# Two head groups of x in one pass over eight TensorE tiles, with w_val's sum and one residual per batch on GpSimd

## The chip, the core and the metric

The kernel runs on one core of one Trainium2 chip. The metric is device time in microseconds (us); the time before is the median of three runs, 319.11 us (318.81 to 319.12). Every view of the profile is of one profiled execution of the kernel before, whose own time is 318.79 us. A time "at 86.9" is counted from the first instruction of that execution.

The engines, as the profile names them: PE is TensorE's matmuls and PEld its weight loads, DVE is VectorE, ACT is ScalarE, POOL is GpSimd, SP is the engine from whose queue all DMAs are issued. PSUM is the memory that matmuls write, SBUF the one that everything else uses.

## The reference

Inputs: q, k, v of 8 batches x 8 heads x 576 rows x 64; p of 8 x 8 x 32 x 64; float64 weights w_val and w_out of 512 x 512 and conv_w of 5 x 512. (q, k, v and p arrive as float32.)

```python
def sm_attn(qq, kk, vv):
    s = scale * np.matmul(qq, kk.transpose(0, 1, 3, 2))
    a = np.exp(s - np.max(s, axis=-1, keepdims=True))
    a = a / (np.sum(a, axis=-1, keepdims=True) + 1e-09)
    return np.matmul(a, vv)
p_packed = sm_attn(p, k, v)              # 32 packed rows per head
out = sm_attn(q, p_packed, p_packed)     # 576 rows per head
x = out.transpose(0, 2, 1, 3).reshape(B, S, H * D)     # 8 x 576 x 512
for k in range(5):
    gate_pre += conv_w[k] * xp[:, k:k + S, :]          # xp: x behind 4 rows of zeros
gate = 1.0 / (1.0 + np.exp(-gate_pre))
return gate * (x @ w_val) @ w_out
```

## The kernel before

One batch's work is cut into streams, each a Python generator: loads (K, V, Q, P for a batch's tensors, L for the weights), `keys` k, `attn_pack` a, `queries` q, `packed_turned` p, `attn_out` s, `weighted` t, `packed_values` w, `mixed` x, `gate` g, `value` v and `project` o, and once per kernel the weights' conversion from float64 words: `value_weights` W, `conv_weights` C and `out_weights` O. The table ORDER is a list of tokens such as `x0` (one step of `mixed` for batch 0) or `a0.3` (three steps of `attn_pack` for batch 0). A step is what stands between two `yield`s. Each engine is wrapped in `InOrder`, so the order in which the tokens issue instructions is the order in which each engine, and the DMA queue of SP, runs them. What moves work is therefore ORDER together with the code of the streams and the numbers of buffers (NB in SBUF, PSB in PSUM).

The eight heads of a batch are two groups of four (G is 2, g counts them). A group's four heads lie on the partitions 0-31, 32-63, 64-95 and 96-127 of `a2` (the weights of the second attention, transposed) and of `ppd` (the packed rows).

The steps that the change touches:

- `words_of`, `from_double`, `summed`, `value_weights`: w_val comes as pairs of 32-bit words in four chunks of 128 rows. ACT and DVE turn a chunk into a high part (`wv_top`) and a low part (in `wv_words`). PE adds the two through matmuls with the identity (`wv_sum`), ACT copies the sum to `wv`. `wv` is read by `packed_values` (`wp`), which gives `wph` and `wpl`, the operands of `value`.
- `weighted`: DVE sums, takes reciprocals, POOL multiplies (`t<-t,rs`), DVE transposes to `a2` (named a in the profile), ACT and DVE split it into `a2h` and `a2l`.
- `mixed`: for each group and each half of the 576 columns four matmuls of 32 x 64 weights and 288 columns, one per head, write x transposed to one PSUM buffer; ACT copies it to `xp`. Head hl takes the rows 32 hl of TensorE's array and the columns 64 (hl mod 2), so four of the eight tiles of that shape are in use at a time:

```python
xps[D * (hl % 2) : D * (hl % 2) + D, hl // 2, :HS],
pp[heads[hl], g, 0, :],
a2[heads[hl], g, hc],
```

- `gate`: from `xp`, one ACT and four DVE instructions for each of four 128-channel blocks, then tanh on ACT, in the tile `sig`.
- `value`: 12 matmuls per block into one PSUM buffer (`val`), DVE multiplies with the gate (`sig<-sig,val`), ACT rounds to `gvh`, and DVE takes the rest, `gvl<-sig,gvh`.
- `project`: output chunks of 128 rows, 36 matmuls each over `gvh`, `gvl`, `woh` and `wol` (o), copied by ACT and written by DMA. For the last batch five chunks are accumulated side by side.

The PSUM buffers called `big` hold two banks each, and there are two of them: scores (s), `wp`, x and `val` take turns in them. Three `mid` buffers and one `out` buffer serve the rest.

Of the kernel before, what the change touches and what calls it, by code (L numbers as in the profile page):

```python
# [9 lines left out]
F32 = mybir.dt.float32  # L10
U32 = mybir.dt.uint32
F32R = mybir.dt.float32r
AF = mybir.ActivationFunctionType
ALU = mybir.AluOpType
# [25 lines left out]
 'xp': 2}  # L40
# [66 lines left out]
def packed_attention_gated_conv(  # L107
# [38 lines left out]
    DM = H * D  # L146
# [27 lines left out]
    eps = const.tile([P, G * NBLK], F32, name="eps")  # L174
# [56 lines left out]
    def from_double(nm, words, rows):  # L231
# [6 lines left out]
        yield  # L238
        dve.tensor_scalar(hw, hw, 1 << 31, None, op0=ALU.bitwise_and)
# [167 lines left out]
    def weighted(b):  # L407
# [5 lines left out]
        for gs in parts(b):  # L413
# [4 lines left out]
            dve.tensor_tensor(s3, s3, eps[:, : n * NBLK], op=ALU.add)  # L418
# [32 lines left out]
    def mixed(b):  # L451

        for g in range(G):
# [3 lines left out]
            for half in range(2):  # L457
                hc = slice(half * HS, half * HS + HS)
                pp, a2 = st["ppd", b], st["a2", b]
                xps = big(f"x_{b}_{g}_{half}")  # L460
# [8 lines left out]
                yield  # L469
                act.copy(xp[:, :, half, PAD:], xps[:, :, :HS])  # L470
# [32 lines left out]
    def value(b):  # L503
        base = (b % 2) * S
        wph, wpl, ah, al = (st[nm, b] for nm in ("wph", "wpl", "ah", "al"))
        for n4 in range(NC):
            vps = big(f"val_{b}_{n4}")
            cols = slice(n4 * P, n4 * P + P)
            for half in range(2):
                hc = slice(half * HS, half * HS + HS)  # L510
                n = 0
                for g in range(G):
                    for w, x in ((wph, ah), (wpl, ah), (wph, al)):
                        pe.matmul(
                            vps[:, half, :HS], w[:, g, cols], x[:, g, hc], start=(n == 0), stop=(n == 5)
# [10 lines left out]
            dve.tensor_tensor(  # L526
# [119 lines left out]
```

## Time and profile before

| | |
|---|---|
| median of three runs | 319.11 us |
| the profiled execution: time, span from first to last instruction | 318.79 us, 316.7 us |
| busy, of the span: PE, DVE, ACT, POOL | 292.0, 256.5, 211.1, 44.8 us |
| granted TensorE clock, mean | 0.997 |
| HBM read, written | 33.57 MB, 9.44 MB |

How to read it: a matmul's busy time runs from its start to its modelled end, and neighbours overlap in it. Where the prediction needs the time that a step takes up on an engine it uses the chain of work that ended last, whose pieces do not overlap: each line there is a start, a length and what ran. A row of the groups by line gives operation, output and inputs by their names in the program, shapes, count, busy time in all, the mean of one in ns, and the idle time before them with what ended it. A row of the table by stretches gives the stretch, its length, each engine's busy time with its number of instructions, the granted clock, the share of the DMA engines and GB/s. All instructions bear line 90, that of the helper that issues them, so the names tell them apart. A matmul in float32 is two instructions in the profile: x8 is four matmuls.

### The profile page before, as it was taken

How to read it: one execution, taken by the hardware profiler on the slowest of the kernel's cores; microseconds unless marked ns; L12 is line 12 of the kernel's file. 1: busy time of each engine (PE TensorE's matmuls, PEld its weight loads, DVE VectorE, ACT ScalarE, POOL GpSimd, SP SyncE). 2: the span in 40 equal slices, each digit the busy share in tenths (PEclk: the TensorE clock that was granted, in tenths of full speed). 3: DMA queues.
4: the chain of work that ended last, by engine and by line, in shares of the span. 5: the costliest groups of instructions: out<-in, count | busy, mean ns of one | idle time of the engine just before them, and what ended most of it. 6: DMA issues, size and time to landing. Idle time of an engine off the chain costs nothing.

```text
span 316.7 us, 7391 instructions
## 1 busy us (share of the span) xinstructions
PE 292.0 (92%) x3028; PEld 210.3 (66%) x3028; DVE 256.5 (81%) x404; ACT 211.1 (67%) x428; POOL 44.8 (14%) x55
## 2 busy tenths in 40 slices
PE   0878987988899999999999999999999999999992
PEld 0534534556766876787777867777787687767871
DVE  0336799999888987898999888997999878868761
ACT  1564787688966778768867786688766955455431
POOL 1000131113002210033003202210032100220000
PEclk9999999999999999999999999999999999999998
DMA  8999999999991479328652866415242021111005
GB/s 180 220 231 226 243 256 218 214 229 192 192 198 74 107 188 224 83 81 216 151 139 73 208 185 120 123 55 129 58 141 68 2 66 36 66 68 47 20 2 167
DMA packets 42476, 43.50 MB, mean 137 GB/s; under 512 B 6085, under 2 KB 36805, under 8 KB 42442
## 3 DMA queue, kind: packets, MB, share of 16 engines
q1 hardware_dynamic: 42442, 43.02, 58.8%
q8 instruction: 24, 0.39, 0.6%
q14 instruction: 10, 0.08, 0.1%
HBM read 33.57 MB, written 9.44 MB: 136 GB/s over the span
## 4 chain that ended last, share of the span: by engine, by line
PE 69%; DVE 15%; ACT 6%; DMA 5%; issue 1%; SPq 0%; POOL 0%; POOLq 0%; DVEq 0%; ACTq 0%
PE o L90 26%; PE val L90 13%; DVE sig L90 6%; PE s L90 5%; PE x L90 5%; PE kpt L90 4%; PE qpt L90 4%; PE pv L90 3%; DMA qm<-in_q_dram 3%; PE at L90 3%; PE wv_sum L90 2%; PE wp L90 2%; DMA p<-in_p_dram 2%; DVE sm L90 2%; ACT sig L90 2%; DVE wo_words L90 1%
## 5 line engine op out<-in xcount | busy, mean ns | idle before, releaser
L90 DVE SCALAR_TENSOR_TENSOR sig<-xp,cw,sig 128x576 f32<-128x576 f32 x128 | 107.5, 840 | 5.9 <-ACT sig L90 4.8
L90 PE MATMUL o<-woh,gvh 128*128 128x512 f32 x144 | 59.0, 409 | 0.1
L90 PE MATMUL o<-wol,gvh 128*128 128x512 f32 x144 | 56.5, 393 | 0.0
L90 PE MATMUL o<-woh,gvl 128*128 128x512 f32 x144 | 56.5, 392 | 0.1
L90 PE MATMUL val<-a2h,wph 128*128 128x288 f32 x128 | 39.9, 312 | 0.0
L90 POOL TENSOR_TENSOR t<-t,mx 128x576 f32<-128x576 f32 x16 | 22.9, 1432 | 110.3 <-DVE mx L90 110.3
L90 PE MATMUL val<-a2h,wpl 128*128 128x288 f32 x128 | 37.9, 296 | 0.0
L90 PE MATMUL val<-a2l,wph 128*128 128x288 f32 x128 | 37.8, 295 | 0.0
L90 ACT COPY osb<-o 128x512 f32<-128x512 f32 x34 | 19.9, 584 | 25.1 <-PE o L90 17.0
L90 ACT ACTIVATE sig<-sig 128x576 f32<-128x576 f32 x32 | 22.0, 689 | 21.3 <-DVE sig L90 21.3
L90 DVE SCALAR_TENSOR_TENSOR sig<-sig,val 128x576 f32<-128x576 f32 x32 | 24.0, 751 | 12.6 <-ACT sig L90 7.8
L90 PEld LDWEIGHTS o<-woh,gvh 128*128 128x128 f32 x144 | 27.1, 188 | 8.8 <-ACT osb L90 2.4
L90 PEld LDWEIGHTS o<-woh,gvl 128*128 128x128 f32 x144 | 27.1, 188 | 6.7 <-DVE gvl L90 0.5
L90 PEld LDWEIGHTS o<-wol,gvh 128*128 128x128 f32 x144 | 27.1, 189 | 4.6
L90 PEld LDWEIGHTS kpt<-ident,km 96*128 96x128 f32 x192 | 20.2, 151 | 11.9 <-issue 4.8
L90 ACT COPY qT<-qpt 128x384 f32<-128x384 f32 x48 | 23.2, 486 | 6.8 <-PE qpt L90 6.5
L90 ACT CAST gvh<-sig 128x576 fp32r<-128x576 f32 x32 | 21.6, 676 | 9.0 <-DVE sig L90 7.9
L90 POOL TENSOR_TENSOR t<-t,rs 128x576 f32<-128x576 f32 x16 | 19.9, 1244 | 54.6 <-DVE rs L90 47.3
L90 PE MATMUL kpt<-ident,km 96*128 96x96 f32 x192 | 25.7, 266 | 2.0 <-DVE wol L90 1.0
L90 DVE TENSOR_TENSOR gvl<-sig,gvh 128x576 fp32r<-128x576 f32 x32 | 24.6, 769 | 2.5 <-ACT gvh L90 2.3
L90 PEld LDWEIGHTS val<-a2h,wph 128*128 128x128 f32 x128 | 24.2, 189 | 2.7 <-issue 0.9
L90 ACT COPY kT<-kpt 128x384 f32<-128x384 f32 x48 | 22.9, 483 | 4.2 <-PE kpt L90 4.0
(82 smaller groups left out, 504.9 us busy)
## 6 DMA issues: line engine op xcount, KB each, us to landing
km<-in_k_dram SPq DMA_DIRECT2D x16, 576.0 KB, 6.1
qm<-in_q_dram SPq DMA_DIRECT2D x16, 576.0 KB, 7.0
vm<-in_v_dram SPq DMA_DIRECT2D x16, 576.0 KB, 7.3
out_dram<-osb SPq DMA_DIRECT2D x24, 256.0 KB, 2.1
wv_words<-in_moe_w_val_dram SPq DMA_DIRECT2D x8, 256.0 KB, 9.1
wo_words<-in_moe_w_out_dram SPq DMA_DIRECT2D x4, 512.0 KB, 13.6
out_dram<-osb SPq DMA_DIRECT2D x8, 192.0 KB, 3.4
p<-in_p_dram SPq DMA_DIRECT2D x16, 64.0 KB, 7.9
```

The lines of the kernel that those rows point to most:

```text
L90: made = getattr(self.engine, op)(*args, **kw)
```

## The change

- `mixed` issues both groups for one half in one step, each group into a PSUM buffer of its own, the second group with its two column halves swapped (`at = D * ((hl + g) % 2)`). The eight matmuls so name all eight tiles of 32 rows x 64 columns. ACT copies the two buffers in two further steps. `xp` has three buffers instead of two, `mx2` two instead of three, and `eps` half its size.
- The channels of group 1 lie swapped by this; the rows or columns of w_val, conv_w and w_out are swapped to match, as they are loaded (`halves`, two small DMAs for conv_w) or written (`wv`).
- `value_weights`: the sum of the two parts is two POOL additions of 128 x 256 per chunk instead of two matmuls and an ACT copy.
- `value`: for the first of the four blocks (n4 is 0) `gvl` is computed by POOL, for the others by DVE as before.
- ORDER is another table from the first token to the last.

`from_double` also gets two arguments that no call uses.

```diff
- 'xp': 2}
+ 'mx2': 2,
+ 'xp': 3}
...
-x0 K0.2 P0 L0.2 Q0 L0.2 V0.2 k0 Q0 L0 k0.2 P1 k0.4 P2 W0 k0.2 W0 K1 k0.2 a0 W0 k0.2 W0 a0 k0 K1 W0.2 a0 W0 L0 a0
+x0 L0 x0 K0 L0 P0 L0 K0 W0 L0 W0.2 P1 W0.2 L0 W0 V0 W0 Q0 V0 W0 k0 Q0 W0 k0.2 P2 W0 k0.2 W0 L0 k0.2 W0.2 K1 k0
...
+    def halves(c):
+        return (c * P, c * P + D) if c < NC // 2 else (c * P + D, c * P)
...
-        st["words", "cw"] = words_of("cw", [conv_w], NT)
+        st["words", "cw"] = words_of("cw", [conv_w[:, : DM // 2]], NT, DM // 2)
+        swapped = conv_w[:, DM // 2 :].bitcast(U32).rearrange("n (c t d) -> n c t d", c=2, t=2)
+        to = st["words", "cw"][:, DM // 2 :, :].rearrange("n (c t d) x -> n c t (d x)", c=2, t=2)
+        for t in range(2):
+            sp.dma_start(to[:, :, t], swapped[:, :, 1 - t])
...
-            st["words", "wo"][c] = words_of(f"wo{c}", [w_out[c * P : c * P + P, :]], P)
+            st["words", "wo"][c] = words_of(f"wo{c}", [w_out[r : r + D, :] for r in halves(c)], P)
...
-            ps = summed(f"wv{c}", words)
-            yield
-            act.copy(wv[:, c, :], ps)
+            for low in range(2):
+                cs = slice(low * DM // 2, low * DM // 2 + DM // 2)
+                to = wv[:, c, cs].rearrange("a (x t d) -> a x t d", x=2, t=2)
+                ins = [
+                    x[:, cs].rearrange("a (x t d) -> a x t d", x=2, t=2)
+                    for x in (st["top", f"wv{c}"], words[:, :, 0].bitcast(F32))
+                ]
+                pool.tensor_tensor(to[:, :, ::-1] if low else to, *ins, op=ALU.add)
...
+        for half in range(2):
+            hc = slice(half * HS, half * HS + HS)
+            pp, a2 = st["ppd", b], st["a2", b]
+            xps = [big(f"x_{b}_{g}_{half}") for g in range(G)]
+            for g in range(G):
                 for hl in range(4):
+                    at = D * ((hl + g) % 2)
                     pe.matmul(
-                        xps[D * (hl % 2) : D * (hl % 2) + D, hl // 2, :HS],
+                        xps[g][at : at + D, hl // 2, :HS],
...
+            for g in range(G):
+                act.copy(st["xp", b, g][:, :, half, PAD:], xps[g][:, :, :HS])
                 yield
...
-            dve.tensor_tensor(
+            (pool if n4 == 0 else dve).tensor_tensor(
                 lo, gv, hi.bitcast(F32), op=ALU.subtract
             )
```

How the instructions stand, at three places. First PE at the start, from the second attention product of batch 0's first group (`pv_0`) on: `at` are transposes for it, `qpt` and `pTt` transposes of q and p, `ppTt` that of the packed rows, `s_0_0` the scores that begin batch 0's second attention, `wp` the product with w_val. Before:

```order
L90 MATMUL at_1_2_306<-ident,a_0_1_223 96x128 x2
L90 MATMUL pv_1_310<-vm_1_103,a1t_1_294 32x64 x24
L90 MATMUL wv_sum<-wv_top,ident 128x512
L90 MATMUL wv_sum<-wv_words,ident 128x512
L90 MATMUL qpt_1_0_350<-ident,qm_1_108 128x96 x4
L90 MATMUL ppTt_356<-ident,ppd_226 128x128 x2
L90 MATMUL pTt_359<-ident,p_120 128x128 x2
L90 MATMUL qpt_1_1_369<-ident,qm_1_108 128x96 x4
L90 MATMUL s_0_0_379<-qT_0_199,ppT_363 32x288 x8
```

And now:

```order
L91 MATMUL at_1_2_329<-ident,a_0_1_241 96x128 x2
L91 MATMUL cwps<-ident,cw_top 128x5 x4
L91 MATMUL pv_1_338<-vm_1_122,a1t_1_317 32x64 x24
L91 MATMUL ppTt_365<-ident,ppd_244 128x128 x2
L91 MATMUL qpt_1_0_373<-ident,qm_1_128 128x96 x4
L91 MATMUL s_0_0_380<-qT_0_294,ppT_370 32x288 x8
```

The last `wv_sum` no longer stands between `pv_1` and `ppTt`, and one `qpt` instead of two and `pTt` stands ahead of the scores.

Second, PE in batch 6 around its x (`x_0_1` is group 0, half 1; `pv`, `at` and `qpt` there belong to batch 7, `val` to batch 5). Before:

```order
L90 MATMUL x_0_1_3300<-a_6_3164,ppd_2670 64x288 x4
L90 MATMUL pv_0_3307<-vm_0_2903,a1t_0_3255 32x64 x24
L90 MATMUL qpt_1_1_3335<-ident,qm_1_3104 128x96 x4
L90 MATMUL at_1_0_3344<-ident,a_7_1_3237 96x128 x2
L90 MATMUL wp_3347<-wv,ppT_3062 32x512 x8
L90 MATMUL x_1_0_3364<-a_6_3164,ppd_2670 64x288 x4
```

And now:

```order
L91 MATMUL val_1_3272<-a2l_2685,wph_2678 128x288
L91 MATMUL x_0_0_3287<-a_6_3147,ppd_2648 64x288 x4
L91 MATMUL x_1_0_3288<-a_6_3147,ppd_2648 64x288 x4
L91 MATMUL pv_0_3299<-vm_0_2886,a1t_0_3122 32x64 x24
L91 MATMUL x_0_1_3327<-a_6_3147,ppd_2648 64x288 x4
L91 MATMUL x_1_1_3328<-a_6_3147,ppd_2648 64x288 x4
L91 MATMUL val_2_3343<-a2h_2684,wph_2678 128x288
```

The four x of a batch, which stood apart, stand in two pairs with only `pv_0` between them, and `val` directly ahead of and behind them.

Third, POOL from batch 6's last multiplication (`t<-t,rs`) to the end. Before:

```order
L90 TENSOR_TENSOR t_6_3068<-t_6_3068,rs_6_3163 128x576
L90 MEMSET xp_1_3356 128x4x2
L90 MEMSET xp_0_3467 128x4x2
L90 TENSOR_TENSOR t_7_3564<-t_7_3564,mx_7_3565 128x576
L90 TENSOR_TENSOR t_7_3564<-t_7_3564,rs_7_3635 128x576
L90 TENSOR_TENSOR t_7_3564<-t_7_3564,mx_7_3565 128x576
L90 TENSOR_TENSOR t_7_3564<-t_7_3564,rs_7_3635 128x576
L90 MEMSET xp_1_3718 128x4x2
```

And now:

```order
L91 TENSOR_TENSOR t_6_3055<-t_6_3055,rs_6_3146 128x576
L91 TENSOR_TENSOR gvl<-sig_0_2945,gvh 128x576
L91 MEMSET xp_0_3361 128x4x2
L91 TENSOR_TENSOR t_7_3430<-t_7_3430,mx_7_3431 128x576
L91 TENSOR_TENSOR t_7_3430<-t_7_3430,rs_7_3510 128x576
L91 MEMSET xp_1_3532 128x4x2
L91 TENSOR_TENSOR gvl<-sig_0_3368,gvh 128x576
L91 TENSOR_TENSOR t_7_3430<-t_7_3430,mx_7_3431 128x576
L91 TENSOR_TENSOR t_7_3430<-t_7_3430,rs_7_3510 128x576
L91 TENSOR_TENSOR gvl<-sig_0_3685,gvh 128x576
```

Three `gvl` (of the batches 5, 6 and 7) have come into the queue, and batch 7's second subtraction stands behind batch 6's `gvl`.

More of the change, by code (lines that the diff above doesn't have):

```diff
@@ new lines @@
+t4 a5 k6 a5 q5 k6 o2 v3 q5 t4 g3 v3 t4 x4 g3 o2 t4 k6 o2 v3 q5 x4 K7 a5 g3 x4 Q6 v3 t4 a5 k6 q5 g3 a5 v3 g3 x4
+v3 V6 a5.3 v3 k6 x4 a5.2 v3 a5 g4 k6 g4 x4 x5 a5 v3 k6 a5.2 k6 g4 v3 k6 g4 a5 a6 V6 k6 K7 p5 v3 k7 o3 p5 a6 g4
+a6 g4.2 s5 o3 g4 a6 o3 s5 o3 k7 a6 s5 a6 g4 s5 a6 g4 w5 o3.2 s5.2 a6 w5 t5 k7 q6 o3 a6 k7 g4 t5 q6 s5 g4 w5 g4
+x5 q6 g4 o3 v4 q6 o3 t5 g4 t5 o3 s5 g4 s5 t5 q6 s5 k7 Q7 a6 q6 t5 o3 q6 a6 o3.2 q6 g4 t5 k7 v4 g4.2 t5 v4 a6 g4
+o3 x5 v4 t5 o3 g4 k7 a6.2 x5.3 V7 a6 k7.2 a6 x5 g4 a6 q6 k7 v4 t5 q6 a6 g4 x5 k7 g4 x6 v4 a6 q6 g5 Q7 v4 g5 k7
@@ L79 @@
+v6.2 o5 g6 o5 t7 g6 o5 g6 v6 t7 g6 v6.3 o5 g6 o5 t7 x7 g6 t7 g6 x7.2 t7 x7 g6 x7 v6 x7 v6 g7 v6 o6 g7 v7 o6 g7
+o6 g7 o6 g7.3 v7 g7 v7 o6 g7 v7.2 o6.2 g7.2 o6 g7 o6.2 g7 v7 g7 v7.3 g7 o6 g7 o6 o7 g7.3 v7 g7 v7 o7 v7 g7.3 o7
+g7 v7 o7 v7.3 o7.15
 """
@@ L173, in packed_attention_gated_conv @@
     heads = [slice(NP * hl, NP * hl + NP) for hl in range(4)]
-    eps = const.tile([P, G * NBLK], F32, name="eps")
+    eps = const.tile([P, NBLK], F32, name="eps")
     nc.gpsimd.memset(eps, 1e-9)
@@ L204, in load_q, with words_of @@
         yield from load(b, "q", q, "h (a i c) d -> i h a (c d)")
-    def words_of(nm, src, rows):
+    def halves(c):
+        return (c * P, c * P + D) if c < NC // 2 else (c * P + D, c * P)
+    def words_of(nm, src, rows, cols=DM):
         words = tile_of("words", [P, DM, 2], U32, f"{nm}_words", stage)[:rows]
@@ L212, in words_of @@
             sp.dma_start(
-                words[n * each : n * each + each].rearrange("a b c -> a (b c)"), s.bitcast(U32)
+                words[n * each : n * each + each, :cols].rearrange("a b c -> a (b c)"), s.bitcast(U32)
             )
@@ L227, in load_weights, with from_double @@
         for c in range(NC):
-            st["words", "wo"][c] = words_of(f"wo{c}", [w_out[c * P : c * P + P, :]], P)
+            st["words", "wo"][c] = words_of(f"wo{c}", [w_out[r : r + D, :] for r in halves(c)], P)
             yield
-    def from_double(nm, words, rows):
+    def from_double(nm, words, rows, by=1.0, rest_on_pool=False):
         top = st["top", nm] = tile_of("top", [P, DM], F32, f"{nm}_top", stage)[:rows]
@@ L238, in from_double @@
         yield
+        if rest_on_pool:
+            act.mul(rest, lw, 2.0**-52 * by)
+            yield
         dve.tensor_scalar(hw, hw, 1 << 31, None, op0=ALU.bitwise_and)
@@ L246, in from_double @@
         yield
-        dve.scalar_tensor_tensor(
-            rest, lw, 2.0**-52, hw.bitcast(F32), op0=ALU.mult, op1=ALU.mult
-        )
+        if rest_on_pool:
+            pool.tensor_tensor(rest, rest, hw.bitcast(F32), op=ALU.mult)
+        else:
+            dve.scalar_tensor_tensor(
+                rest, lw, 2.0**-52 * by, hw.bitcast(F32), op0=ALU.mult, op1=ALU.mult
+            )
         yield
@@ L417, in weighted @@
             dve.tensor_reduce(s3, t3, axis=AX.X, op=ALU.add)
[L418 removed]
+            dve.tensor_tensor(s3, s3, eps, op=ALU.add)
             dve.reciprocal(r3, s3)
@@ L456, in mixed @@
             yield
[L457 to L460, printed above, removed]
+        for half in range(2):
[3 more added lines that the diff above has]
+            for g in range(G):
                 for hl in range(4):
+                    at = D * ((hl + g) % 2)
                     pe.matmul(
-                        xps[D * (hl % 2) : D * (hl % 2) + D, hl // 2, :HS],
+                        xps[g][at : at + D, hl // 2, :HS],
                         pp[heads[hl], g, 0, :],
@@ L468, in mixed @@
                     )
-                yield
-                act.copy(xp[:, :, half, PAD:], xps[:, :, :HS])
+            yield
+            for g in range(G):
+                act.copy(st["xp", b, g][:, :, half, PAD:], xps[g][:, :, :HS])
                 yield
@@ L514, in value @@
                         pe.matmul(
-                            vps[:, half, :HS], w[:, g, cols], x[:, g, hc], start=(n == 0), stop=(n == 5)
+                            vps[:, half, :HS], w[:, g, n4 * P : n4 * P + P], x[:, g, hc], start=(n == 0), stop=(n == 5)
                         )
```

55 lines of the change are left out of this document (23 added, 32 removed).

## The prediction

> **What bounds the kernel now.** I read the page's busy times first, then the table by stretches, then the chain of waits, to see which wait ends last in each stretch.
>
> ```profile
> PE 292.0 (92%) x3028; PEld 210.3 (66%) x3028; DVE 256.5 (81%) x404; ACT 211.1 (67%) x428; POOL 44.8 (14%) x55
> ```
>
> The same by stretches of the span (us; busy us and count of PE, PEld, DVE, ACT, POOL; clock; DMA share; GB/s):
>
> ```profile
> 0.00:36.00 36.00, 23.37 (x242) 12.61 (x242) 14.45 (x29) 16.47 (x37) 0.80 (x8) 1.00 1.05 218
> 36.00:85.00 49.00, 42.82 (x535) 26.45 (x528) 46.56 (x83) 40.25 (x89) 10.81 (x10) 1.00 1.08 219
> 85.00:272.00 187.00, 186.96 (x2034) 142.34 (x2033) 166.35 (x253) 135.02 (x273) 28.48 (x32) 1.00 0.48 119
> 272.00:308.00 36.00, 35.83 (x218) 26.73 (x217) 27.78 (x40) 17.56 (x28) 4.69 (x5) 1.00 0.11 37
> 308.00:317.00 9.00, 3.06 (x13) 2.18 (x13) 1.39 (x2) 1.76 (x3) 0.00 (x0) 0.88 0.46 147
> ```
>
> There are three regimes. Up to 36 nothing is full but the DMA engines: it is the start, a chain of loads and short dependent steps. From 36 to 85 DVE is full (46.56 of 49), so whatever lets DVE begin sooner moves all of it. From 85 to 308 PE is full (222.8 of 223); there time is won by taking instructions from PE, and DVE has 20.7 of 187 us to spare.
>
> **The start.** The chain there:
>
> ```profile
> 29.97 2.12 PE wv_sum L90 x4
> 32.75 0.44 PE pTt L90 x2
> 33.19 0.49 PE qpt L90 x4
> 33.68 1.11 PE s L90 x16
> 35.27 1.10 PE wp L90 x16
> 37.44 1.23 DVE wpl L90
> ```
>
> The last sum of w_val holds PE for 2.12 us in front of the transposes (`ppTt`) on which batch 0's second scores (s at 33.68) hang. In the new order no sum is there, and `wv` is made by DVE and POOL while PE waits for loads. What is late next is q and v of batch 0. The view of the tensor qm and the SP queue give their landing in batch 0:
>
> ```profile
> 13.56 0.31 SPq L90 DMA_DIRECT2D qm<-in_q_dram  x1
> DMA to landing us min/median/max: 11.4/13.1/14.9
> ```
>
> The second q tile, issued at 13.56, lands at the latest at 13.56 + 14.9 = 28.5, and `vm_1`, queued just ahead of it, before that. The new queue has the same bytes up to there plus one more p (two loads of 64 KB), which at 218 GB/s is 0.6 us. With `vm_1` between 26 and 28.5 there follow `pv` 0.81, `ppd` 0.37, two transposes and their copy, each below 0.5 (`pTt` row), so some 2.4 us: s starts between 28.7 and 31. I take 29.7, the middle rounded down, since `qT` for it is ready earlier: **4.0 us gained**, with 2.7 and 5.0 as ends. After it, DVE is full again and carries the 4.0 us through to where PE is full.
>
> The additions themselves: eight on POOL, whose queue holds nothing else ahead of batch 0's subtraction. The trace has no POOL addition of 128 x 256; its nearest row is the 128 x 576 multiplication below, 1.24 us, so eight cost at most 10 us of POOL, and by size 8 x 0.55 = 4.4. The last chunk's words are the fourth load pair of the new queue, behind 3.4 MB (four pairs of 512 KB, two k tiles, one p), 16 us at 218 GB/s; with some us to land, the conversion and the last two additions the sums end by 25, and `wp` needs them after 30. Cover: 5 us. I put them at 0. Gone from ACT are four copies of 0.58 us, which nobody waits for any more.
>
> **The x pairs.** PE just where it becomes full, from the chain, whose pieces do not overlap:
>
> ```profile
> 85.11 1.60 PE val L90 x12
> 86.93 0.64 PE x L90 x8
> 87.57 0.81 PE pv L90 x48
> 88.38 0.65 PE x L90 x8
> 89.64 1.60 PE val L90 x12
> 91.24 2.78 PE o L90 x12
> 94.01 1.13 PE s L90 x32
> 98.09 0.65 PE s L90 x16
> ```
>
> A group's half of x (x8) takes 0.65 us. The scores s have the same 288 columns on eight tiles of 64 x 32, and sixteen instructions of them (x16) take 0.65 us as well: twice the matmuls in the same time. So a pair of x, sixteen instructions on eight tiles, should take 0.65 instead of 2 x 0.65. The x alone, in the same two stretches:
>
> ```profile
> 85.00:272.00 187.00, 15.73 (x176) 4.54 (x176) 14.15 (x22) 1.00 0.48 119
> 272.00:308.00 36.00, 2.86 (x32) 0.82 (x32) 2.53 (x4) 1.00 0.11 37
> ```
>
> 208 instructions, 26 groups of eight, become 13 pairs: 13 x 0.65 = **8.4 us gained** where PE is full. The other six groups lie in the DVE-bound stretch and gain nothing. The ends: 0 (four tiles at a time, as now) and 8.4.
>
> What speaks against it: no row shows four row blocks writing into one column half at once; s and today's x have two. [...]
>
> **The new wait.** A pair takes both `big` buffers at once, and they are the only two. It must wait until DVE or ACT has emptied what was in them, and what comes next in them waits for the copies:
>
> ```profile
> L90 ACT COPY xp<-x 128x576 f32<-128x576 f32 x32 | 20.6, 642 | 0.3
> L90 DVE SCALAR_TENSOR_TENSOR sig<-sig,val 128x576 f32<-128x576 f32 x32 | 24.0, 751 | 12.6 <-ACT sig L90 7.8 <-PE val L90 4.4
> ```
>
> Where two copies (1.28) or one emptying of `val` (0.75) is longer than the PE work in between, PE stands. By the new order: batch 1 has `pv` (0.81) and `pTt` (0.22) between its pairs and only `ppTt` behind, about 0.7; batch 2 has one `at` between `val_2` and its second pair, 0.5; batches 3 to 5 some 0.6 together; batch 6 has nothing between `val_1` and its first pair (0.75), `pv` alone between the pairs (0.5), nothing before `val_2` (0.65); batch 7 has `val_3` directly ahead (0.75) and the pairs back to back (1.3). Sum 5.8. Part of it is shorter, since a copy starts while the group behind it still runs, and queued PE instructions begin as soon as one buffer is free. The ends are 0 and 16.6 (each of 13 pairs waiting for both copies); nearer the counted sum, I take **3.0 us lost**.
>
> **gvl on POOL.** DVE and POOL where both run (timeline of each):
>
> ```profile
> 205.24 1.25 DVE L90 SCALAR_TENSOR_TENSOR sig<-xp,cw,sig 128x576 f32<-128x576 f32 x1
> 208.24 0.72 DVE L90 SCALAR_TENSOR_TENSOR sig<-xp,cw,sig 128x576 f32<-128x576 f32 x1
> ```
>
> ```profile
> 204.70 1.16 POOL L90 TENSOR_TENSOR t<-t,mx 128x576 f32<-128x576 f32 x1 [0.51 <-DVE mx L90]
> 208.47 1.51 POOL L90 TENSOR_TENSOR t<-t,rs 128x576 f32<-128x576 f32 x1 [2.60 <-DVE rs L90]
> ```
>
> The gate's sum that started during POOL's 1.16 took 1.25, not 0.72, and ended 0.6 after POOL; POOL's that started during a sum took 1.51. They take turns. [...] So a `gvl` taken from DVE saves these rows' 0.77 us of DVE and gives back up to 0.5:
>
> ```profile
> L90 DVE TENSOR_TENSOR gvl<-sig,gvh 128x576 fp32r<-128x576 f32 x32 | 24.6, 769 | 2.5 <-ACT gvh L90 2.3
> L90 POOL TENSOR_TENSOR t<-t,rs 128x576 f32<-128x576 f32 x16 | 19.9, 1244 | 54.6 <-DVE rs L90 47.3 <-ACT kT L90 4.1 <-ACT qT L90 3.2
> ```
>
> Batch 0's lies in the DVE-bound stretch: 0.7 gained less 0.2. Six lie where PE is full, where DVE's spare time hides both gain and loss: 0. Batch 7's lies in the last chain of DVE, which the gate's sums fill: 0.3 gained to 0.4 lost, taken as 0. Sum **0.5 gained**. What queues behind each is batch-wise subtraction and multiplication on POOL; POOL is busy 28.48 of 187 us, so I put this at 0 and carry the case where it isn't as a rival.
>
> **The end.** The chain there:
>
> ```profile
> 284.43 0.79 ACT sig L90
> ...
> 307.00 0.77 DVE gvl L90
> 307.82 3.26 PE o L90 x13
> 311.10 0.58 ACT osb L90
> ```
>
> Today DVE's gate and PE end together, at 307.8. In the new order batch 7's scores come with more of batch 6 still to do on both. Behind the last pair PE has four chunks o at 2.78, four `val` at 1.60 and five accumulated chunks (some 13.9), 31.4 us; DVE's sixteen sums, multiplications and waits for tanh, then the last product, are what took from 284.4 to 311.1 before, 26.7. PE still ends it, so what it saved before counts. The third `xp` and the two `mx2` cost 0: ACT never waited for `xp` (idle 0.3 in the row above).
>
> **Sum.** 318.79 - 4.0 - 8.4 + 3.0 - 0.5 = 308.9. The profiled execution lies 0.32 below the median of 319.11, so I say 309.2, in round terms 309.
>
> **Rivals.**
> - *The pairs are no faster.* The four row blocks of a column half take turns; the pair takes 1.3. That gives back 8.4, and about 2 of the wait, since a longer pair covers part of it: 315.6. For it: no row shows the form. Against: s. [...]
> - *The hand-over of the two buffers costs more.* DVE is 89% busy, and where its emptying of `val` is late the second group of a pair starts late too, and the pair isn't a pair. At 1.28 for half of the 13 pairs more than I took, 8 us: 317. Against: PE waited nowhere for `big` in this order's forerunner (186.96 of 187).
> - *Slower.* POOL runs in order, and `gvl` must wait for ACT's `gvh`, which waits for `val`. Behind it stand the next batch's subtraction or multiplication, which lead through DVE's `a` to that batch's x. If this makes each of the six batches from 1 to 6 wait, it eats the whole gain from 9.9 / 6 = 1.65 us per batch on; at 2.5 us per batch the time is 309.2 + 15 = 324. For it: POOL's multiplications wait 47 us for DVE today, so they are on time-critical ground. Against: the spare time of DVE, 20.7 us over 5.5 batches (176 x of 32 each), 3.8 per batch.
> - *Better than forecast.* No waits, the start at its best: 309.2 - 3 - 1 - 0.5 = 304.5, and with less idling in the DVE-bound stretch 303.
>
> **How the numbers follow.** The forecast (304 to 312) has 0.68, the pairs no faster 0.13, the hand-over 0.08, slower 0.07, better than 304 0.04. The range 303.5 to 316.5 holds the forecast, the better case's near part and most of the two middle rivals. A measurement of this kernel can tell about 0.2% (0.6 us) from no change. Faster: 0.68 + 0.04 + 0.13 + 0.04 (half of the hand-over) = 0.89; within 0.2%: 0.03 from the hand-over's far end; slower: 0.07 + 0.01.
>
> **What would show it.** In the chain after: x x16 with 0.65 to 0.7 (right) or 1.3 (no concurrency), x16 in place of every x8; s of batch 0 near 29.7; no `wv_sum`. In the waits: PE for ACT `xp` and DVE `sig`, 3 us in all, more in batches 6 and 7 than elsewhere. In the timeline: gate sums of 1.2 us beside POOL's `gvl`. The stretch in which PE is full should begin near 80 and still be full. The prediction is wrong if PE idles by over 8 us there, which would be the hand-over or POOL's queue, told apart by whether PE's x waits for ACT and DVE emptying `big`, or for DVE `a`.

## The result, and the profile after

The changed kernel takes 333.77 us (median of four runs, 332.22 to 336.8) against 319.12 of the kernel before beside it: a ratio of 1.0472, 95% interval 1.0427 to 1.0518. It is 14.7 us slower, where 10 us faster was forecast. The profiled execution took 333.92 us, its span is 332.1. Medians and ratios leave out executions over 1.5% above the fastest of their kernel. The page's busy times after:

```profile
PE 294.6 (89%) x3012; PEld 216.4 (65%) x3012; DVE 259.3 (78%) x396; ACT 210.7 (63%) x424; POOL 67.0 (20%) x71
```

PE has 16 instructions less and is busy 2.6 us more. The table by stretches (columns as in the prediction), before:

```profile
32.00:96.00 64.00, 57.67 (x715) 36.34 (x714) 59.06 (x101) 49.58 (x107) 10.91 (x11) 1.00 1.07 217
256.00:304.00 48.00, 47.90 (x346) 37.30 (x345) 39.79 (x57) 23.88 (x39) 4.80 (x6) 1.00 0.14 48
```

And after:

```profile
32.00:96.00 64.00, 54.19 (x610) 33.82 (x614) 49.86 (x83) 43.07 (x93) 11.99 (x12) 0.95 0.92 192
...
128.00:256.00 128.00, 127.34 (x1408) 96.47 (x1408) 114.33 (x173) 95.44 (x195) 30.43 (x28) 1.00 0.49 127
256.00:304.00 48.00, 43.85 (x391) 34.54 (x391) 41.34 (x57) 26.39 (x45) 9.58 (x8) 1.00 0.12 39
```

Between 32 and 96, where DVE was full (59.06 of 64), it now does 9.2 us less work. The DMA engines were full there too (share 1.07, 217 GB/s) and now are not (0.92, 192 GB/s). PE is full again from 128 to 256 and has 4 us of pauses behind that. The chain of waits after, at batch 0's second attention:

```profile
23.17 1.55 PE pv L91 x48
24.73 2.15 PE qpt L91 x12
...
28.94 1.48 PE pv L91 x48
...
31.98 1.14 PE s L91 x16
33.12 0.83 PE qpt L91 x4
33.95 1.89 PE wp L91 x16
...
37.24 1.22 PE s L91 x16
38.46 2.11 PE kpt L91 x12
40.57 3.45 PE wo_sum L91 x4
```

No `wv_sum`, as forecast; but `pv` takes 1.5 instead of 0.81, `wp` 1.89 instead of 1.10, a `qpt` x4 0.83 instead of 0.49: PE runs at little more than half the speed of those rows. The chain later on:

```profile
82.63 3.25 PE val L91 x12
...
94.86 0.71 PE x L91 x8
95.57 0.81 PE pv L91 x48
...
96.75 0.69 PE x L91 x8
97.44 0.74 DVE sig L91
98.23 0.71 PE x L91 x8
...
104.34 1.60 PE val L91 x12
```

The `val` at 104.34 is the first of batch 1; before, it stood at 89.64. So 14.7 us are lost by here. From it to the end of the span it is 332.1 - 104.3 = 227.8 us, and before 316.7 - 89.6 = 227.1: behind this place nothing is lost and nothing won. The pairs of batch 1 are also no pairs: x8, a wait for ACT or DVE, x8.

Where DVE lost its time, the timeline of DVE shows at the first gate sum of batch 0, before and then after:

```profile
52.27 0.78 DVE L90 SCALAR_TENSOR_TENSOR sig<-xp,cw,sig 128x576 f32<-128x576 f32 x1
```

```profile
59.37 1.67 DVE L91 SCALAR_TENSOR_TENSOR sig<-xp,cw,sig 128x576 f32<-128x576 f32 x2 [3.67 <-ACT sig L91]
```

It starts 7.1 us later, after a pause of 3.67 in which DVE, whose queue is in order, stands at this sum.

### The profile page after: what moved, and what is told of

The parts are those of the page before. It is cut to its first block, busy times and chain, and to the rows that moved or that the text cites. A ratio compares the mean times of both kernels' runs of the same rounds, so it can differ in the third digit from the quotient of the medians.

```text
span 332.1 us, 7381 instructions
## 1 busy us (share of the span) xinstructions
PE 294.6 (89%) x3012; PEld 216.4 (65%) x3012; DVE 259.3 (78%) x396; ACT 210.7 (63%) x424; POOL 67.0 (20%) x71
## 4 chain that ended last, share of the span: by engine, by line
PE 66%; ACT 12%; DVE 12%; DMA 4%; issue 2%; SPq 1%; ACTq 0%
PE o L91 27%; PE val L91 12%; DVE sig L91 6%; PE qpt L91 5%; PE s L91 4%; PE x L91 4%; PE pv L91 3%; ACT sig L91 3%; PE kpt L91 3%; DMA wv_words<-in_moe_w_val_dram 2%; PE at L91 2%; PE wo_sum L91 2%; DMA cw_words<-in_moe_conv_w_dram 2%; PE wp L91 2%; ACT xp L91 2%
## 5 line engine op out<-in xcount | busy, mean ns | idle before, releaser
L91 DVE SCALAR_TENSOR_TENSOR sig<-xp,cw,sig 128x576 f32<-128x576 f32 x128 | 112.2, 877 | 11.7 <-ACT sig L91 10.6
L91 DVE SCALAR_TENSOR_TENSOR sig<-sig,val 128x576 f32<-128x576 f32 x32 | 23.9, 746 | 18.7 <-PE val L91 11.1
L91 POOL TENSOR_TENSOR t<-t,rs 128x576 f32<-128x576 f32 x16 | 21.6, 1350 | 51.3 <-DVE rs L91 40.6
L91 PEld LDWEIGHTS qpt<-ident,qm 96*128 96x128 f32 x192 | 21.1, 153 | 10.9 <-issue 6.6
L91 ACT CAST gvh<-sig 128x576 fp32r<-128x576 f32 x32 | 21.6, 676 | 9.6 <-DVE sig L91 9.0
L91 PE MATMUL qpt<-ident,qm 96*128 96x96 f32 x192 | 26.7, 269 | 0.1
## 6 DMA issues: line engine op xcount, KB each, us to landing
wo_words<-in_moe_w_out_dram SPq DMA_DIRECT2D x8, 256.0 KB, 11.7
```

The lines of the kernel that those rows point to most:

```text
L91: made = getattr(self.engine, op)(*args, **kw)
```

## The experiments

In all of them "old" and "new" are the ORDER or the code of the kernel before and of the changed one. Ratios are to the kernel before, run beside it on the same chip.

### PE's speed, the pairs' tiles, and w_val on POOL

PE kept busy from the start:

```diff
     make_identity(nc, ident)
+    warm = one("warm")
+    for _ in range(30):
+        pe.matmul(warm[:, :P], ident, ident, start=True, stop=True)
```

> The changed kernel with 30 products of the identity with itself on PE ahead of everything (1.4 to about 11 us, while PE waits for the first load); nothing else differs. Theory 1 (cold PE): in the changed kernel PE's instructions take 1.7 to 2 times as long from 11.3 to 43 us as they do later, because PE idles until 11.3 and then never works long enough at a stretch to get up to speed. The pieces of PE in the chain of waits between 23 and 44 us add up to 17.5 us; at the later durations they would be 10. So a warm PE should bring s of batch 0 from 32.0 to 30 and the whole from 333.8 to 325 to 329. Theory 2 (order): the loss up to 104 us is waits that the new order makes between the engines, whatever PE's speed; then at most 2 us are won, 332 to 334. If the speed falls back after the first pause, both give about 333.

Measured: 333.92 us, 1.0449 (1.0400 to 1.0497), no change. The speed came and went again, as PE's timeline shows:

```profile
13.02 1.19 PE L91 MATMUL kpt<-ident,km 96*128 96x96 f32 x12
15.61 1.21 PE L91 MATMUL s<-kT,pT 64*32 64x288 f32 x16 [1.41 <-ACT kT L91]
```

The twelve `kpt` instructions at 13.0 take 1.19 us, but the scores at 15.6, behind a pause of 1.41, take 1.21 instead of 0.65 to 0.72. So this run does not tell the theories apart. The second one keeps PE at work further on, in the same place as the POOL additions:

```diff
             yield from from_double(f"wv{c}", words, P)
+            summed(f"wv{c}", words)
             for low in range(2):
```

> The changed kernel with the eight matmuls of the sums of w_val on PE as well, in the place of the POOL additions; their result is not used. Theory 1 (cold PE): the added work between 10 and 28 us fills PE's pauses and PE comes up to speed there instead of at 43; later pieces (wp, s, kpt, wo_sum) are then short, 326 to 332 in spite of 8 us more work. Theory 2 (order): the sums only add a PE wait for the conversion of w_val, 334 to 340.

Measured: 330.62 us, 1.0358 (1.0294 to 1.0422). PE is fast through most of the start in its trace (`wp` at 34.4 takes 1.09), and four useless sums of 2.0 to 3.6 us each bring a gain of 3.2 us, a fifth of the loss. PE's low speed is a part of the loss; how large it would be without the work of the sums was not measured.

```diff
-                    at = D * ((hl + g) % 2)
+                    at = D * (hl % 2)
```

> The changed kernel with group 1 of x on the same two column halves as group 0 in the same order, so that a pair uses four tiles and not eight (group 1's channels stay unswapped, so the gate belongs to other channels; order, sizes and counts are the same). If the eight tiles run at the same time, each of the 13 unsplit pairs should take 1.3 instead of 0.7 and the time rise by 4 to 8 us, to 338 to 342. If the waits for the two buffers split nearly all pairs, or if PE has enough slack, it rises by less than 2 us.

Measured: 334.63 us, 1.0462 (1.0393 to 1.0531): no difference from the changed kernel. The chain shows why. Of the changed kernel:

```profile
193.34 0.76 PE x L91 x16
221.50 0.67 PE x L91 x16
223.46 1.17 PE x L91 x16
```

And of the kernel on four tiles, the same three pairs:

```profile
193.56 1.13 PE x L91 x16
221.91 1.13 PE x L91 x16
224.33 1.13 PE x L91 x16
```

Eight tiles do run at the same time: 0.67 and 0.76 instead of 1.13. But the third pair takes 1.17 on eight tiles too, since its second group waits for a buffer (ACT copies the pair before out of it until 223.86), and in batches 1, 2, 3 and 7, and once in batch 6, the chain shows groups singly. What is won is too little, and too seldom on the path, to be measured.

w_val on POOL alone, in the old order:

```diff
-            ps = summed(f"wv{c}", words)
-            yield
-            act.copy(wv[:, c, :], ps)
+            for low in range(2):
+                cs = slice(low * DM // 2, low * DM // 2 + DM // 2)
+                ins = (st["top", f"wv{c}"][:, cs], words[:, cs, 0].bitcast(F32))
+                pool.tensor_tensor(wv[:, c, cs], *ins, op=ALU.add)
+            yield
             yield
```

> The kernel before with one part of the change alone: w_val added by POOL (two additions of 128 x 256 per chunk) in place of eight matmuls and four ACT copies; the order of all else as before. Theory 1 (cold PE): without the sums PE has longer pauses between 14 and 32 us and works at half speed there, so this part alone loses: 320 to 326. Theory 2 (order): it gains what the removed sum ahead of the scores held PE, 1 to 3 us, 316 to 318.

Measured: 319.21 us, 0.9988 (0.9968 to 1.0008): no change. PE was slow here too, its `wp` takes 1.97 where the kernel before takes 1.10. And yet s of batch 0 comes 2.7 us earlier than before (33.68), since no sum stands ahead of it:

```profile
31.00 1.14 PE s L90 x16
...
32.97 1.97 PE wp L90 x16
...
63.40 10.09 DMA km<-in_k_dram
...
89.70 1.60 PE val L90 x12
```

Nothing of these 2.7 us is left at batch 1's first `val`, 89.70 against 89.64. The first gate sum still comes 1.5 us earlier (50.77 against 52.27); behind it the chain of waits runs through a load of 10.09 us, as the chain before runs through one of q, 9.66 us from 53.90. So this one run tests the prediction's step from an earlier start to an earlier end, in the old order, and the step does not hold. It does not tell what a slow PE costs by itself, since the sums went at the same time.

### Order against parts

The four corners: the changed kernel and the kernel before are two of them, and these two the others. New ORDER, old code:

```diff
-x0 K0.2 P0 L0.2 Q0 L0.2 V0.2 k0 Q0 L0 k0.2 P1 k0.4 P2 W0 k0.2 W0 K1 k0.2 a0 W0 k0.2 W0 a0 k0 K1 W0.2 a0 W0 L0 a0
...
+x0 L0 x0 K0 L0 P0 L0 K0 W0 L0 W0.2 P1 W0.2 L0 W0 V0 W0 Q0 V0 W0 k0 Q0 W0 k0.2 P2 W0 k0.2 W0 L0 k0.2 W0.2 K1 k0
...
+                    at = D * (hl % 2)
```

> The changed kernel's ORDER with the code of the kernel before: w_val summed by PE and copied by ACT (in one step), gvl all on DVE, the weights unswapped; the two groups of x still stand in one step with a buffer each, but on four tiles. Theory 3 (the order itself): the new sequence of instructions makes PE, ACT and DVE wait for each other up to 104 us, whatever the parts are; then this is as slow as the changed kernel, 328 to 336. Theory 4 (the parts on POOL): the additions of w_val and the gvl on POOL are what is late; then this comes near the kernel before, 318 to 323.

Measured: 338.35 us, 1.0576 (1.0511 to 1.0641). Old ORDER, new code, x group by group:

```diff
-x0 L0 x0 K0 L0 P0 L0 K0 W0 L0 W0.2 P1 W0.2 L0 W0 V0 W0 Q0 V0 W0 k0 Q0 W0 k0.2 P2 W0 k0.2 W0 L0 k0.2 W0.2 K1 k0
...
+x0 K0.2 P0 L0.2 Q0 L0.2 V0.2 k0 Q0 L0 k0.2 P1 k0.4 P2 W0 k0.2 W0 K1 k0.2 a0 W0 k0.2 W0 a0 k0 K1 W0.2 a0 W0 L0 a0
...
+                xps = big(f"x_{b}_{g}_{half}")
```

> The kernel before's ORDER with the new parts but for the pairs: w_val added by POOL, gvl of the first 128 channels on POOL, three xp and two mx2 tiles, the swapped weights with their extra DMAs; x is issued group by group as before, in the swapped halves. Theory 3 (the order): within 1% of the kernel before, 317 to 321. Theory 4 (the parts on POOL): most of the loss, 326 to 334.

Measured: 319.48 us, 1.0004 (0.9971 to 1.0038). That settles the first question. The additions and the `gvl` on POOL, the third `xp` and the extra DMAs together cost and bring nothing in the old order; the new order, with the two groups of x in one step, loses 18.6 us with the old code and 14.7 with the new.

The two tables cut at batch 1's first `val` and joined crosswise:

```diff
+x0 K0.2 P0 L0.2 Q0 L0.2 V0.2 k0 Q0 L0 k0.2 P1 k0.4 P2 W0 k0.2 W0 K1 k0.2 a0 W0 k0.2 W0 a0 k0 K1 W0.2 a0 W0 L0 a0
...
 s2 g1 t2 g1.2 s2 v1 o0 t2 g1 o0 v1 a3 o0 v1 k4 s2 a3 s2 a3 g1 s2 k4 o0 q3 a3 k4 a3 g1 o0 w2 q3 a3 s2 q3 o0 t2 w2
```

> All new parts, with the old ORDER up to the first step of batch 1's value (x of batches 0 and 1 group by group) and from there the new ORDER (x in pairs from batch 2 on). Theory 3a (the early order): in the profiles the changed kernel is 14.7 us behind at val_0 of batch 1 and no further behind at the end, so this gets back to 317 to 321. Theory 3b (the late order): the loss is made behind that point too, and only masked by what the pairs save; then 323 to 330.

Measured: 324.20 us, 1.0129 (1.0074 to 1.0183).

```diff
 x0 L0 x0 K0 L0 P0 L0 K0 W0 L0 W0.2 P1 W0.2 L0 W0 V0 W0 Q0 V0 W0 k0 Q0 W0 k0.2 P2 W0 k0.2 W0 L0 k0.2 W0.2 K1 k0
...
+o0 g1 s2 v1 o0 k4 a3 g1 a3.2 x2 q3 v1 s2 a3 s2 a3 t2 q3 k4 v1 w2 k4 s2 t2 g1 k4 v1 q3 w2 v1 s2 k4 q3 w2 s2 k4 q3
```

> All new parts, with the new ORDER up to the first step of batch 1's value and from there the old ORDER (x of batches 2 to 7 group by group). Theory 3a (the early order): the 14.7 us are lost up to there and stay lost: 331 to 337. Theory 3b (the late order): 320 to 326.

Measured: 334.31 us, 1.0461 (1.0411 to 1.0511). The early order alone loses all of it, as the profile said. The late order loses 4.4 us behind an old early part, which was theory 3b's case, and nothing behind a new one, which was theory 3a's: the losses do not add.

### What a pair costs

Old ORDER and new code, with x of batches 0 and 1 in pairs; batch 0's tokens behind its second group's weights:

```diff
-t0 O0 g0 a1 t0 x0 O0.2 g0 a1.6 O0 x0 g0 x0 a1 V2 t0 p1 v0 g0 p1 x0
+t0 O0 a1 t0 x0.4 O0.2 a1.6 O0 a1 V2 t0 p1 x0.3 g0.4 v0 g0 p1
```

> Old ORDER with the new parts, and x of batches 0 and 1 in pairs: each pair stands where group 1's first half stood, the second pair some 1.5 to 2.6 us of other PE work later, and the gate's first instructions of that batch behind it (batch 0: three sums later). Theory 5 (pairing ties group 0 to group 1): in the profile of the changed kernel the first gate sum of batch 0 starts at 59.4 instead of 52.3, since both groups' weights must be there first, and DVE stands idle 3.7 us ahead of it. Then this alone costs part of the 14.5 us, 322 to 328. Rival 6 (the rest of the early order: loads, conversions, what stands between): no change, 318 to 321.

Measured: 331.74 us, 1.0375 (1.0342 to 1.0407). Twelve us for four pairs and the gate instructions that had to follow them: theory 5 is right that pairing loses, and the loss is above its range. In this kernel's view of waits DVE stands 18.5 us for ACT's `sig`, against 12.6 without the pairs, and the granted clock from 32 to 64 us is 0.77 against 0.95; what the slower PE adds was not tested apart. The converse, in the changed kernel:

```diff
-O0 k1.2 t0 k1.2 K2 k1 O0.2 t0 s0 w0 O0 s0 O0.2 a1 s0 O0 k1 t0 k1.2 O0 t0 a1 k1.2 K2 k1 k2 P4 O0 a1 t0
+O0 k1.2 t0 k1.2 K2 k1 O0.2 t0 s0 w0 O0 s0 O0.2 a1 s0 O0 k1 t0 k1.2 O0 t0 a1 x0.2 k1.2 K2 k1 k2 P4 O0 a1 x0.2 t0
```

> The changed kernel with x of batch 0 group by group: group 0's two halves and their copies right behind the first steps of the scores that follow its weights, group 1's where the pairs stood, and the first product of the gate's first block on ACT ahead of the wait. Theory 5: DVE's gate sums can begin 3 to 7 us earlier and fill its pause at 55.7 to 59.4; 327 to 331. Rival 6: the first sums only move into the pause and the next wait takes its place, 332 to 335.

Measured: 330.89 us, 1.0369 (1.0323 to 1.0415), some 3 us better than the changed kernel, whose interval begins at 1.0427. That is the slow end of theory 5's range, a fifth of the loss. The profiled execution, at 333.98 us, shows what rival 6 says: the first two sums start at 57.1, and then DVE stands 3.2 us at `wol`, which waits for ACT and that for PE's `wo_sum`. So the place of the first sums is a part of the loss, and the trace does not show where the 3 us come from.

The same edit in batches 2 to 7, here batch 2:

```diff
-x2.2 Q4 a3 v1 g2 a3 x2 g2 x2 V4 a3 v1 a4 g2 x2
+x2.4 Q4 a3 v1 a3 V4 a3 v1 a4 x2.3 g2.3
```

> Old ORDER with the new parts, and x of batches 2 to 7 in pairs where group 1's first half stood, with other PE work between the two pairs of a batch (1.4 to 3.4 us by its durations). PE is full there, and a pair takes 0.7 where two groups take 1.3: twelve pairs by 0.6 are 7 us at most. If the pairs are worth what a PE-bound stretch says, 312 to 316; if waits for the two buffers or DVE take it back, 318 to 321; slower, 322 to 326, if the new waits exceed it, as they do in the run with the old early and the new late order (324.2).

Measured: 358.08 us, 1.1208 (1.1168 to 1.1248). None of the three expectations: 38 us lost where PE was full and the pairs should save PE work. Both pairs of batch 3 are split here, too: PE's x8 start at 155.89 and 157.31, and at 161.00 and 162.47. Around batch 3's pairs, ACT's timeline and then DVE's:

```profile
163.25 0.64 ACT L92 COPY xp<-x 128x576 f32<-128x576 f32 x1 [0.83 <-PE x L92]
163.78 0.78 ACT L92 ACTIVATE sig<-xp,cw 128x576 f32<-128x576 f32 x1
```

```profile
159.59 0.76 DVE L92 TENSOR_TENSOR gvl<-sig,gvh 128x576 fp32r<-128x576 f32 x1 [1.42 <-ACT gvh L92]
164.60 0.82 DVE L92 SCALAR_TENSOR_TENSOR sig<-xp,cw,sig 128x576 f32<-128x576 f32 x1 [4.25 <-ACT sig L92]
```

DVE has finished batch 2's gate and stands 4.25 us until both halves of the next x are copied. To tell this from the hand-over of the buffers, the next run leaves x as it stood and moves the gate's first instructions alone:

```diff
-x2.2 Q4 a3 v1 g2 a3 x2 g2 x2 V4 a3 v1 a4 g2 x2
+x2.2 Q4 a3 v1 a3 x2.2 V4 a3 v1 a4 x2 g2.3
```

> Old ORDER, new parts, x group by group where it stood, and only the first one to seven gate instructions of batches 2 to 7 moved behind the place where the second pair stood in the run with late pairs (358.1). Theory 9 (DVE starves): what cost 38 us there is that DVE's next gate sums cannot start before both groups' x are copied, while PE goes on; then the move alone costs most of it, 340 to 358. Rival 10 (the hand-over of the two PSUM buffers in PE): the move alone costs little, 319 to 326.

Measured: 341.11 us, 1.0709 (1.0669 to 1.0749). Moving up to seven gate instructions per batch (and in batch 7 its first `val`) a few places back, with no pair at all, costs 21.6 us over the old order with the new parts. The DVE rows of the views of waits, of that kernel without the move, with it, and with the pairs (us in total, times, longest):

```profile
DVE sig L93 <- ACT sig L93: 12.6, 19, 1.0
```

```profile
DVE sig L92 <- ACT sig L92: 30.0, 24, 7.2
```

```profile
DVE sig L92 <- ACT sig L92: 45.3, 25, 7.8
```

Theory 9 is right for the greater part of the 38 us. The other 17 us of the pairs came with x itself moved; the two buffers were not tested apart from that.

### Which half of the early order

The tables joined at batch 0's second scores instead, first the old start:

```diff
+K0.2 P0 L0.2 Q0 L0.2 V0.2 k0 Q0 L0 k0.2 P1 k0.4 P2 W0 k0.2 W0 K1 k0.2 a0 W0 k0.2 W0 a0 k0 K1 W0.2 a0 L0 a0 W0 q0
...
 k1 O0 k1.2 t0 k1.2 K2 k1 O0.2 t0 s0 w0 O0 s0 O0.2 a1 s0 O0 k1 t0 k1.2 O0 t0 a1 k1.2 K2 k1 k2 P4 O0 a1 t0 a1 O0.2
```

> All new parts, with the old ORDER up to the first scores of batch 0's second attention (s_0_0, 32 us) and from there the new ORDER. Theory 7 (the middle: 32 to 104 us, where x of batches 0 and 1 is paired): the loss stays, 328 to 334. Theory 8 (the start: loads and w_val ahead of batch 0, PE late and slow): it goes, 320 to 326.

Measured: 333.43 us, 1.0455 (1.0415 to 1.0496): theory 7. Then the new start:

```diff
 L0 K0 L0 P0 L0 K0 W0 L0 W0.2 P1 W0.2 L0 W0 V0 W0 Q0 V0 W0 k0 Q0 W0 k0.2 P2 W0 k0.2 W0 L0 k0.2 W0.2 K1 k0 W0 a0
...
+k1.4 a1 k1 s0 t0 k1 O0 a1 k1 k2 K2 O0 a1.2 P4 t0 O0 t0 x0 a1 k2 q1 O0 a1.3 O0.2 a1 s0 q1 x0 t0 s0 O0 q1 a1 O0.2
```

> All new parts, with the new ORDER up to the first scores of batch 0's second attention and from there the old ORDER, x group by group in all batches. Theory 7: near the kernel before, 318 to 323. Theory 8: 328 to 334.

Measured: 332.04 us, 1.0411 (1.0358 to 1.0464): theory 8. Both hold, since either half alone loses nearly everything; the first of the two runs has the late order as well. With the new start the chain of waits runs through loads of batches 0 and 1 (q, k and q again, 10.4 to 11.7 us each, from 18.67 to 51.58). Next, the changed kernel with PE filled at 77 to 82 us too:

```diff
+    def fill(b):
+        for n in (5, 3, 3):
+            t = one("fill", "out")
+            for _ in range(n):
+                pe.matmul(t[:, :P], ident, ident, start=True, stop=True)
+            yield
```

> The changed kernel with the sums of w_val on PE as well (unused, as in the earlier run, 330.6) and eleven more products of the identity with itself on PE in the three pauses between 77 and 82 us, ahead of the products val that took 3.25 us instead of 1.6 at a granted clock of 0.65 to 0.78. If the low clock there costs what the slow pieces show (val 1.65, pv 0.6 and some transposes), 327 to 329; if it only hides behind the other waits, 330 to 331.

Measured: 329.68 us, 1.0369 (1.0292 to 1.0445), not different from the 330.62 (1.0358) without the fill: no gain shown, and the interval is too wide to exclude one of 2 us.

Then the loads alone, first into the old order, then the old ones into the new:

```diff
-x0 K0.2 P0 L0.2 Q0 L0.2 V0.2 k0 Q0 L0 k0.2 P1 k0.4 P2
+x0 L0 K0 L0 P0 L0 K0 L0 P1 L0 V0 k0 Q0 V0 k0.2 Q0 k0.4 P2
```

> Old ORDER, new parts, x group by group; only the sequence of the loads in the DMA queue is the new one (four chunks of w_val among and ahead of batch 0's k, p, v and q). Theory 11 (the loads make the start's loss): batch 0 and with it everything up to 85 us comes later by what stands ahead of its tensors, 324 to 332. Rival 12 (the places of the compute steps make it): 318 to 322.

```diff
-x0 L0 x0 K0 L0 P0 L0 K0 W0 L0 W0.2 P1 W0.2 L0 W0 V0 W0 Q0 V0 W0 k0 Q0
+x0 K0 x0 K0 P0 L0.2 Q0 W0 L0 W0.2 L0 W0.2 V0 W0 V0 W0 Q0 L0 W0 k0 P1
```

> The changed kernel with the old sequence of loads in the places of the new ones. Theory 11 alone would bring it back by some us, 322 to 330, if the middle with its pairs did not lose as much by itself; as the run with the old start and the new rest took 333.4, theory 7 expects 331 to 335 here.

Measured: 330.41 us, 1.0339 (1.0277 to 1.0401), for the new loads in the old order, theory 11; and 349.43 us, 1.0917 (1.0838 to 1.0997), for the old loads in the new order, which is slower than any of the expectations. Either sequence loses in the other's order, 11 and 16 us. In the first, the chain of waits runs through a load of batch 1:

```profile
40.40 10.12 DMA qm<-in_q_dram
50.57 0.90 PE qpt L93 x4
51.47 0.43 PE at L93 x2
51.90 3.10 PE wo_sum L93 x4
55.01 0.61 ACT woh L93
```

PE stands at a transpose of batch 1's q while `wo_sum`, whose operands are there, is queued behind it, and ACT and DVE behind that. The changed kernel's view of waits has no row of PE waiting for q; there the steps stand where their loads come.

## Why the prediction was wrong

**The start, -4.0.** s of batch 0 came from 33.68 to 31.98, 1.7 instead of 4.0. What was late next was not v or q, as I had it, but PE at little more than half speed: the second `pv` starts at 28.94 because PE gets to it only then, with no wait for v, and it and the pieces around it take up to 1.8 times the durations of the kernel before that I used (`pv` 1.48 for 0.81, `wp` 1.89 for 1.10). In the trace PE is slow at first and fast at 43.9 (`s` x16 takes 1.21 us at 19.65 and 0.72 at 43.94), and slow once more at 82.63 (`val` 3.25 instead of 1.60); what sets its speed no run shows by itself. I took the sums of w_val out of PE and kept the durations of a PE that had them: `wp` takes 1.09 with the sums put back, and 1.97 in the old order without them. The step that failed altogether is the next sentence, "DVE is full again and carries the 4.0 us through": it carries an early start through only if its own queue has work ready in that order. In the new one DVE was busy 49.86 of 64 us instead of 59.06. This is the main error. I read the new order at the three places of the diff and took the rest, up to 85 us, to be the old stretch moved forward. In the old order DVE does not carry an early start through either: with w_val on POOL s came 2.7 us earlier, and batch 1's `val` and the end did not. From 36 to 85 DVE was not the only thing full: my own row of that stretch has the DMA engines at 1.08 and 219 GB/s, and I used that column only up to 36. That the loads are what holds the old order there is likely by its chain of waits, but no run shows it by itself. (Two small sums are off: 26 and 2.4 make 28.4, not 28.7, and the better case comes to 304.7, not 304.5. Neither matters here.)

**The x pairs, -8.4.** Eight tiles work at once (0.67 to 0.76 for a pair, against 1.13 on four), so the rival "no faster" fell. But the sum needed every pair unsplit and a full PE. Busy time of x fell by 3.7 us, from 22.9 to 19.2, and four tiles instead of eight make no measurable difference. That "the other six groups lie in the DVE-bound stretch and gain nothing" hid the loss: with group 0's x tied to group 1's weights, DVE's gate starts later. Four such pairs in the old order, with the gate behind them, cost 12 us, in another placing than the changed kernel's.

**The new wait, +3.0.** Counted at PE it was nearly right in kind: PE's rows for x in the view of waits after are

```profile
PE x L91 <- ACT xp L91: 3.3, 4, 1.0
PE x L91 <- DVE sig L91: 1.7, 3, 0.8
PE x L91 <- DVE a L91: 1.3, 1, 1.3
```

5.0 us for the two buffers in the first two rows, near the 5.8 before I cut it. What I did not count is who needs the pair: the gate on DVE. I took DVE's 20.7 us of spare time for slack that any wait may use; the run with the moved gate loses 21.6 us with PE's work unchanged. In the changed kernel itself this is one wait among several: DVE's wait for ACT's `sig` grew from 12.6 us to 15.4, that for PE's `val` from 4.4 to 11.1, that for the scores from 1.9 to 5.5.

**gvl on POOL, -0.5, and w_val on POOL, 0.** Right to within what can be measured: 319.48 with both in the old order. `gvl` takes 1.67 us on POOL (the nearest row I had showed 1.24), and it is hidden:

```profile
L91 POOL TENSOR_TENSOR gvl<-sig,gvh 128x576 fp32r<-128x576 f32 x8 | 13.3, 1668 | 21.5 <-ACT gvh L91 21.2 <-DMA vm<-in_v_dram 0.3
```

POOL does wait 21 us for `gvh` as the slower rival said. In the old order it waits 85 us for it, and what waits for POOL's subtractions and multiplications in turn is 0.9 us there and 4.9 in the changed kernel (ACT and DVE, for `t`). So the case on the slow side had the wrong mechanism for most of the loss; the time of 324 it gave was too low as well.

**The end, 0.** From batch 1's `val` on the two kernels take the same time: what x saves on PE is no more than the pauses behind 256 us, 4.15 us of 48.

The step that failed is thus the one from the start to the end: I put the cost of a whole new order up to 85 us at nothing, and by the runs that order loses all of the 14.7 us (334.31 with the old order behind it, 319.48 with the new parts in the old order). What stays open is how the 14.7 us divide. PE's speed is worth 3 or more, the place of batch 0's x about 3. The new start, the sequence of the loads (which the new start has, up to 32 us) and early pairs each lose 11.5 to 13.1 when put into the old order alone, and the old start saves nothing in the new one, so they are not terms of a sum.

## What to carry to other kernels

Where each engine runs its queue in a fixed order, an order is one part and not a list of places: loads, conversions and steps fit each other, and a run with the new order and the old code (or the reverse) tells in one pair what the order itself is worth. DVE, 89% busy from 85 to 272 us in the kernel before (166.35 of 187), had no slack to spend at the place where it is handed its next batch of work (21.6 us lost with the gate's first instructions moved), so a step that joins two producers must be followed to the consumer on the busiest engine. Where several columns of a stretch are full, here DVE (46.56 of 49 us) and the DMA engines (1.08), an earlier start on one of them was no gain yet (2.7 us at batch 0's s left 319.21). Before durations are taken from a trace for an order in which PE has less to do, ask whether PE will still run at the speed of those rows (`wp` took 1.10 before and 1.89 after).

## What was not expected of the hardware

PE lost its speed behind short pauses: in the run with the early products `kpt` x12 takes 1.19 us at 13.02 and 2.15 at 17.34, and none of the pauses ahead of it was longer than 2.55 us; transposes ran between them. And in the changed kernel PE had work from 28.4 to 36.7 us without a pause, in small tiles and transposes, and stayed slow (`kpt` x12 2.18 at 38.39) until 43.9, when the four instructions of `wo_sum` on the full array had run (`kpt` x12 1.38 at 44.58). They need not be what raised it: in the old order with w_val on POOL PE was fast from 34.8 on (`kpt` x4 0.55 there, `qpt` x4 0.90 at 32.07), behind 6.6 us of the same small tiles and transposes alone. What took and what raised the speed is not shown. The granted clock in the profile did not show the slow stretch of the changed kernel, ahead of which PE had not been fast (`kpt` x12 2.13 at 11.75). The same 16 us of the changed kernel and of the one with early products, where PE had been fast before, with a `qpt` x12 of 2.15 us in both:

```profile
16.00:32.00 16.00, 14.04 (x168) 10.33 (x176) 8.25 (x19) 8.69 (x22) 3.69 (x4) 1.00 1.15 219
```

```profile
16.00:32.00 16.00, 13.14 (x170) 9.26 (x154) 8.81 (x19) 7.78 (x20) 3.95 (x5) 0.50 1.09 217
```

1.00 in the one and 0.50 in the other: here, at the start of the program, the durations tell PE's speed, and the column does not.
